# Attention and a Mish FFN in one kernel: two units' probabilities computed with keys on partitions, and a new order of the work

## The chip, the cores and the metric

The kernel runs on one core of one Trainium2 chip. The metric is the device time of one execution in microseconds. In the profile PE is TensorE (PEld its weight loads), DVE VectorE, ACT ScalarE, POOL GpSimd, and SP SyncE, which issues most DMAs.

## What is computed

Attention over 8 batches, 8 heads, 576 tokens and 64 dimensions, four heads with a plain window of 32 tokens, four with every fourth token of a window of 128; then a feed-forward layer on all 4608 tokens, 512 to 2048 to 512, whose weights come as 64-bit floats:

```python
def _attn_ref(q, k, v):
    scores = scale * np.matmul(q, k.transpose(0, 1, 3, 2))
    mask_plain = (rel >= 0) & (rel < window)
    mask_dil = (rel >= 0) & (rel < window * dilation) & (rel % dilation == 0)
    scores = np.where(masks[None, :, :, :], scores, -1000000000.0)
    scores = scores - np.max(scores, axis=-1, keepdims=True)
    attn = np.exp(scores)
    attn = attn / (np.sum(attn, axis=-1, keepdims=True) + 1e-09)
    return np.matmul(attn, v).astype(np.float32)

def _moe_ref(x, w_in, w_out):
    h = x @ w_in
    sp = np.where(h > 20.0, h, np.log1p(np.exp(np.minimum(h, 20.0))))
    g = h * np.tanh(sp)
    return (g @ w_out).astype(np.float32)
```

## The kernel before, in words

The work is cut into 16 **units**, one for each batch and half of the tokens (288 tokens). In a unit the eight heads are four **pairs**: pairs 0 and 1 plain (planar), pairs 2 and 3 dilated. For each pair `scores_of_pair` (step sp) puts a mask product (L650) and q·k (L653) into a double PSUM bank, queries on partitions; `scores` (sc) takes the maximum nm (L683) and, for most pairs, subtracts it (L685); `exps` (ex) does the exponentials; `transpose_p` (tp) brings the probabilities to keys on partitions; `values` (va) multiplies them with v (L801) and divides by the sum (L824, L825); `transpose_x` (tx) brings the result x to the layout of the feed-forward layer, as a half-precision high part (L853) and a low part (L858).

Units 0 to 2 are **direct**: scores in fp32, the probabilities transposed by PE (L778) and copied by ACT into one of two buffers pp (L787). In unit 0 PE itself subtracts the maximum in PSUM (L705) before the exponential (L711); in others a BIASED set does the exponential block by block (L718). From unit 3 on the scores' operands are split into half-precision parts and the probabilities go through a DMA transpose (L771). The feed-forward layer is ff1 (L1054, `ff`), Mish by `gate` (gt, L1069 and L1071), and ff2 (L1081, `fo`), each product as three half-precision ones. From unit 4 on two units share a first layer of seven products for eight, from forms that `w_forms` writes to DRAM (L900 to L918) and `x_forms` makes of x (L939).

The weights pass once through preparation, piece by piece (eight pieces of the first layer, eight of the second): `w_load` (wl), `w_max` (wm, ACT L391, the high words scaled into the place where the weights will stand), `w_scale` (ws, PE L402 and a few small DVE steps), `w_words` (ww, three DVE passes L434, L436, L437 that put a 32-bit float together of the two words; the last sets the sign), `w_split` (wp, ACT L446 and DVE L449). `prep` (pr) finds the scale of v in the direct units by DVE maxima (L334).

The order of everything is one long table, ORDER, of steps by name with a PSUM bank or buffer behind the equals sign, run down once by a loop; a step that is a generator stands in it once for each of its parts. Each engine works through its own instructions in that order, and waits in place. `kw` entries are zero matmuls on PE (`keep_warm`, L1110): there are 328, all ahead of the first ff1. There are four double PSUM banks, four raw weight buffers, two pp and two xs. SP issues the DMAs in the table's order.

Of the kernel before, what the change touches and what calls it, by code (L numbers as in the profile page):

```python
# [35 lines left out]
HI = 2.0 ** -112  # L36
MASKED = -2.0 ** 30
# [17 lines left out]
tp1.3=2 ff0.1=0 va1.2=1 ld2 tp1.3=1 wl1.2.1=0 ww0.1.0 wp0.2.1 wp0.1.0 ff0.1 ff0.1 va1.0=0 wm1.2.1 gt0.3 ww0.1.1
va1.3=2 tp1.1=3 tp1.1=0 ww1.2.1 ff0.5=0 ff0.4=3 ff0.4 va1.2 va1.2=1 wl1.2.0=1 wp0.1.1 tx1.0=1 wm1.2.0 wp0.1.0 ff0.5
ff0.4=2 va1.3 tx1.0 ww1.2.0 ff0.5 ws1.2=3 wp0.1.1 fs1 wl1.3.1=3 va1.3=0 tx1.0 tx1.3=0 tx1.3 tx1.0 ff0.2=2 va1.1=1 pr2
tx1.3 ws1.2 gt0.0=1 va1.1 gt0.0 tx1.3 tx1.2=3 tx1.2 va1.1=0 wl1.3.0=2 ww1.2.1 ff0.2 ff0.2=0 sp2.3=0 sc2.3=1 wm1.3.0
ww1.3.0 wm1.3.1 tx1.2 tx1.1=1 tx1.2 tx1.1 tx1.1 wp1.2.1 wp1.2.1 ff0.3=2 ff0.3 ff1.7=3 ff1.7 sp2.1=1 ff0.3 ex2.3 pr2=2
ww1.2.0 pr2 tp2.3=2 ff1.6=0 gt0.2=5 tp2.3=1 sc2.1=3 ww1.3.1 ex2.1 ws1.3=2 ww1.3.0 wp1.2.0 ff1.6 ws1.3 ff1.6=1 ff1.2=1  # L60
wp1.2.0 ff1.2 gt0.1=0 ff1.7 ff1.3=2 wl1.0.0=0 wl1.0.1=1 wm1.0.0 tp2.1=0 ff1.3 gt0.2 tp2.1=0 va2.1=3 ww1.3.1 sp2.2=0
gt0.1 ff1.2=2 ff1.3 sp2.0=1 fo0.2.0=2 ww1.0.0 fo0.2.1 fo0.2.2 gt1.1=2 va2.1 wp1.3.0 sc2.2=0 va2.1=1 wp1.3.1 va2.3=3
fo0.2.3 ex2.2 wp1.3.0 sc2.0=2 wf1.1=0 wl1.1.1=2 gt1.1 va2.3 wm1.0.1 wm1.1.1 wp1.3.1 ff1.1=0 fo0.2.3=0 wl1.1.0=3
va2.3=0 ww1.0.1 xa2.0=4 ws1.0=3 wf1.1 ex2.0 ff1.1 ws1.0 wf1.1=2 wf1.1 tx2.1=1 wf1.1 ff1.0=3 ww1.1.1 tx2.1 wm1.1.0
ww1.1.0 tx2.1 tx2.1 ww1.0.1 ff1.0 ff1.0=0 ff1.5=1 ff1.1 tp2.2=3 ws1.1=0 tp2.2=0 ff1.4=3 wp1.0.1 ww1.0.0 ff1.5 ff1.4
gt1.0=3 ws1.1 lv3 wp1.0.0 fs2 ff1.4=2 fo0.3.0 ff1.5 gt1.2=6 tx2.3=3 tp2.0=0 ww1.1.0 tp2.0=1 va2.2=1 ww1.1.1 xa2.1=0
# [143 lines left out]
def attn_mish_ffn_kernel(  # L210
# [960 lines left out]
```

## Time and profile before

| what | before |
|---|---|
| median of 3 runs (lowest to highest) | 878.14 us (876.85 to 878.18) |
| the profiled execution, its own time | 878.1 us |
| its span in the profile | 876.3 us |
| busy: PE, DVE, ACT | 864.0 (99%), 684.4 (78%), 674.0 (77%) us |

The span is the stretch that the profile covers; the execution's own time has 1.8 us more around it. A busy time of PE counts matmuls that overlap each other, so the length of a group of matmuls is read best from the start of one group to the start of the next. Many fp32 matmuls stand in the profile as two records each.

### The profile page before, as it was taken

What the parts mean: (1) busy time and instruction counts of PE and PEld (TensorE: products, weight loads), DVE (VectorE), ACT (ScalarE), POOL (GpSimd) and SP (SyncE); (2) the same over time, 40 slices, a digit from 0 to 9 for tenths busy, and PEclk for the clock granted to TensorE, in tenths of its full rate; (3) what the DMA queues carried; (4) which work ended last, traced back from release to release, by engine and by line L of the source; (5) the groups of instructions that cost most, each with busy time, mean ns of one, the idle gap of its engine ahead of it and who ended that gap; (6) DMA issues with size and microseconds to landing.
All of it is one profiled execution on the core that took longest, in us unless ns stands there. A gap on an engine that the chain in (4) does not pass through costs nothing.

```text
span 876.3 us, 21569 instructions
## 1 busy us (share of the span) xinstructions
PE 864.0 (99%) x8992; PEld 696.0 (79%) x8996; DVE 684.4 (78%) x1048; ACT 674.0 (77%) x994; POOL 20.7 (2%) x91
## 2 busy tenths in 40 slices
PE   9999999989999999999999999999999999999998
PEld 8878887777888778877888788777887788877776
DVE  5999999999999898988888598977887587743210
ACT  3688997789888999879996989778887759636412
POOL 1000005000000000000000000000000000000000
PEclk9999999999999999999999999999999999999999
DMA  8674362575578876766987767866685654645201
GB/s 278 215 214 158 130 197 59 156 178 151 129 182 205 208 185 179 177 142 186 208 163 158 205 183 169 196 126 166 182 197 153 174 167 113 133 105 181 82 1 55
DMA packets 210865, 141.20 MB, mean 161 GB/s; under 512 B 151376, under 2 KB 195920, under 8 KB 210768
## 3 DMA queue, kind: packets, MB, share of 16 engines
q1 hardware_dynamic: 210768, 139.83, 61.5%
q8 instruction: 70, 1.15, 0.5%
q14 instruction: 27, 0.22, 0.1%
HBM read 93.06 MB, written 16.78 MB: 125 GB/s over the span
## 4 chain that ended last, share of the span: by engine, by line
PE 67%; ACT 5%; DVE 2%; DMA 2%; issue 1%; SPq 1%; DVEq 0%; ACTq 0%
PE b L1081 35%; PE b L966 23%; PE b L807 3%; PE b L1054 3%; PE b L653 2%; DMA w<-wd 1%; DMA pT<-p 1%; ACT hm L976 1%; ACT sb L724 0%; DVE p L768 0%; ACT k L576 0%; ACT p L766 0%; DVE sb L677 0%; ACT hm L1057 0%; DMA vdn<-in_vd 0%
## 5 line engine op out<-in xcount | busy, mean ns | idle before, releaser
L1081 PE MATMUL b<-g,w 128*128 128x288 f16 x3072 | 391.1, 286 | 0.0
L1081 PEld LDWEIGHTS <-w 128*128 128x128 f16 x3072 | 296.7, 98 | 74.5
L966 PEld LDWEIGHTS <-w 128*128 128x128 f16 x2016 | 195.0, 98 | 52.4 <-issue 1.6
L966 PE MATMUL b<-xf,w 128*128 128x288 f16 x1440 | 210.7, 286 | 1.8 <-DMA w<-wd 0.8
L1054 PE MATMUL b<-xf,w 128*128 128x288 f16 x768 | 101.6, 289 | 2.9 <-DVE g L825 2.2
L1071 DVE SCALAR_TENSOR_TENSOR g<-hm,sg,g 128x1152 f16<-128x1152 f32 x64 | 90.0, 1411 | 17.3 <-ACT g L1069 17.3
L1054 PEld LDWEIGHTS <-w 128*128 128x128 f16 x768 | 74.8, 99 | 22.9 <-DVE g L825 2.5
L1095 ACT ACTIVATE y<-b,fo 128x288 f32<-128x288 f32 x60 | 43.9, 739 | 54.2 <-PE b L1081 44.7
L1069 ACT ACTIVATE g<-hm,sg 128x1152 f16<-128x1152 f32 x64 | 79.9, 1253 | 0.9
L976 ACT ACTIVATE hm<-hm,fs 128x576 f32<-128x576 f32 x72 | 53.9, 770 | 18.8 <-DVE hm L1012 13.4
L966 PE MATMUL b<-w,w 128*128 128x288 f16 x288 | 64.4, 286 | 0.0
L768 DVE TENSOR_TENSOR p<-sb,p 96x768 f16<-96x768 f32 (+3 forms) x52 | 46.7, 904 | 14.0 <-ACT p L766 13.9
L685 DVE TENSOR_TENSOR sb<-sb,nm 96x768 f32<-96x768 f32 (+4 forms) x64 | 49.2, 769 | 2.2
L683 DVE TENSOR_REDUCE nm<-sb 96x6 f32<-96x768 f32 (+4 forms) x64 | 48.8, 763 | 1.8
L724 ACT ACTIVATE sb<-sb,ln_p 96x768 f32<-96x768 f32 (+3 forms) x52 | 46.1, 896 | 5.2 <-DVE sb L685 5.0
L766 ACT CAST p<-sb 96x768 f16<-96x768 f32 (+3 forms) x52 | 41.3, 794 | 3.2 <-DMA pT<-p 2.5
L807 PEld LDWEIGHTS <-pT 128*128 128x128 f16 (+3 forms) x1092 | 39.4, 98 | 2.7 <-DMA out_T<-y 0.3
L1027 DVE TENSOR_TENSOR hm<-b,hm 128x576 f32<-128x576 f32 x24 | 18.1, 752 | 27.5 <-PE b L966 26.8
L966 PE MATMUL b<-xg,w 128*128 128x288 f16 x288 | 39.4, 286 | 0.0
L653 PEld LDWEIGHTS <-q 64*72 64x72 f16 (+1 forms) x1092 | 28.1, 116 | 8.1 <-issue 6.7
L949 ACT CAST w<-w 72x1024 f16<-72x1024 f32 (+3 forms) x27 | 23.3, 867 | 14.4 <-DVE w L940 4.1
L951 DVE TENSOR_TENSOR w<-w,w 72x1024 f16<-72x1024 f32 (+3 forms) x27 | 27.0, 999 | 9.2 <-ACT w L949 9.0
(192 smaller groups left out, 1147.3 us busy)
## 6 DMA issues: line engine op xcount, KB each, us to landing
w<-wd SPq DMA_DIRECT2D x84, 512.0 KB
qn<-in_qT SPq DMA_DIRECT2D x16, 576.0 KB
out_T<-y SPq DMA_DIRECT2D x64, 144.0 KB
raw<-in_w_in SPq DMA_DIRECT2D x16, 512.0 KB
raw<-in_w_out SPq DMA_DIRECT2D x16, 512.0 KB
vn<-in_v SPq DMA_DIRECT2D x48, 128.0 KB
wd<-hm SPq DMA_DIRECT2D x32, 128.0 KB
knd<-in_kdT SPq DMA_DIRECT2D x16, 208.0 KB
```

The costliest lines, as they stand in the source:

```text
L653: nc.tensor.matmul(o, q, k, start=start, stop=stop, skip_group_check=True)
L683: nc.vector.tensor_reduce(nm[:nq, :, j:j + n], x, axis=AX.X, op=ALU.max, negate=True)
L685: nc.vector.tensor_tensor(blocked(sb, c0, n, w), x, nm[:nq, :, j:j + n].unsqueeze(3).broadcast_to([nq, 2, n, w]), op=ALU.add)
L724: nc.scalar.activation(x, x, AF.Exp, bias=ln_p[:nq])
L768: nc.vector.tensor_tensor(lo, src, hi, op=ALU.subtract)
L807: nc.tensor.matmul(avv[:, h, j], pp[:nk, c:c + P], vv[vi][:nk, j, hh, :], start=(i == 0), stop=(i == 2))
L966: nc.tensor.matmul(o[:, h, :HT], t[:, c, wi, h * P:(h + 1) * P], form_of(p, x, c, xi), skip_group_check=True, start=start and n == 0, stop ...
L976: nc.scalar.activation(o, src, AF.Mish, scale=U[2 * p]["fs"][:, j:j + 1])
L1054: nc.tensor.matmul(ph[:, h, :HT], w1[j][c // WIDE][:, c % WIDE, wi, k * P:(k + 1) * P], x_of(d, xi, c), start=(n == 0), stop=(n == len(seq ...
L1069: nc.scalar.activation(g[:, 0], m, AF.Identity, scale=sg)
L1071: nc.vector.scalar_tensor_tensor(g[:, 1], m, sg, g[:, 0], ALU.mult, ALU.subtract)
L1081: nc.tensor.matmul(po[:, :HT], w2[:, e, j, wi, k * P:(k + 1) * P], d["g"][j][:, gi, k, :], start=(j == 0 and n == 0), stop=(j == NCH - 1 a ...
```

## The change

- **Units 0 and 1 (ACROSS).** The maximum nm is still found from scores with queries on partitions. Then `across`, called in place of the transposes, computes the scores once more with keys on partitions: for each block and head a mask product with the mask as weights, a k·q product, and a product whose weights are nm spread over the columns and whose other operand is the unit matrix. The exponential goes from PSUM straight into pp. L705, L778 and L787 of these units, their `ex` steps, L711 and L718 go.
- **Their prep (SUMMED).** The scale of v comes of sums of magnitudes, one ACT pass each for v and the dilated v, in place of DVE maxima.
- **Six weight pieces (SIGNED).** `w_max` is a parametric ReLU with a negative slope, so that the sign goes with the word; the third pass of `w_words` goes; a new step `wa` takes the magnitude on ACT for `w_scale`.
- **`transpose_x`** takes two pairs at once: one copy for the high, one for the low part. There are two more xs buffers.
- **Unit 0's loads**: q in two halves; the first half and the planar k come first on SP, then the first weights.
- **`x_forms`** subtracts half as much in one step.
- **ORDER** is another table: 208 zero matmuls in place of 328, 196 of them ahead of the first ff1, 60 in a row at the start.

```diff
-kw4=1 kw4=2 wl0.0.1=0 kw4=2 kw4=0 kw4=3 xa0.1=0 kw4=1 kw4=2 wl0.0.0=1 kw4=0 ld0 kw4=1 kw4=0 kw4=2 kw4=3 kw4=1 kw4=3
...
-BIASED = {(0, 0), (0, 1), (0, 2), (0, 3), (1, 0), (1, 3), (2, 0), (2, 1), (2, 2), (2, 3), (3, 2), (3, 3)}
-ON_PE = {(0, 0), (0, 1), (0, 2), (0, 3), (1, 0), (1, 2), (1, 3), (2, 1), (2, 2), (3, 3)}
+BIASED = {(2, 0), (2, 1), (2, 2), (2, 3)}
+ON_PE = {(0, 0), (0, 1), (1, 0), (1, 1), (2, 1)}
+ACROSS = {0, 1}
+SUMMED = {0, 1}
+SIGNED = {(0, 0, 0), (0, 0, 1), (0, 3, 0), (0, 3, 1), (0, 2, 0), (0, 2, 1)}
 ON_DVE = {(0, 1), (1, 0), (1, 1), (1, 2)}
-PE_SUBTRACTS = {0}
...
+    xss += [t.rearrange("p h c -> p (h c)")[:, :4 * P].rearrange("p (j k) -> p j k", k=P) for t in sbs[2:]]
...
-        nc.scalar.activation(a, hi.bitcast(F32), AF.Identity, scale=HI)
+        if (k, g, p) in SIGNED:
+            nc.scalar.activation(a, hi.bitcast(F32), AF.Prelu, scale=HI, alpha=-SIGN)
+        else:
+            nc.scalar.activation(a, hi.bitcast(F32), AF.Identity, scale=HI)
+
+    def w_abs(k, g, p):
+
+        lo, _ = raws[k, g, p]
+        nc.scalar.activation(w_dst(k, g, p)[:, :, 0].bitcast(BF16), lo.bitcast(F32), AF.Abs)
...
         nc.vector.scalar_tensor_tensor(lo, lo, 29, a, ALU.logical_shift_right, ALU.bitwise_or)
-        nc.vector.scalar_tensor_tensor(lo, hi, -0x80000000, lo, ALU.bitwise_and, ALU.bitwise_or)
+        if (k, g, p) not in SIGNED:
+            nc.vector.scalar_tensor_tensor(lo, hi, -0x80000000, lo, ALU.bitwise_and, ALU.bitwise_or)
...
+        if u == 0:
+            nc.sync.dma_start(qn[:, :2], qT[b, half, :, :2])
...
+        if d["direct"] and not exact:
+            nc.gpsimd.memset(m, 0.0)
+            unused = take("pp", pps).rearrange("p a t -> p (a t)").bitcast(BF16)
+            for x, o, n in ((d["vn"], m[:, 0:1], P), (d["vdn"][:kd], m[:kd, 1:2], kd)):
+                j, h, e = x.shape[1:]
+                magnitudes(o, x, unused[:n, :j * h * e].rearrange("p (j h e) -> p j h e", j=j, h=h))
+            yield
+            mr = yield from largest(m, 2, u)
...
+        if u in ACROSS:
+            yield from across(u, pair)
+            return
...
+    def across(u, pair):
+
+        d = U[u]
+        bl = blocks(d, 2 * pair)
+        nq = bl[0][0]
+        nm, _ = d.pop(("nm", pair))
+        d.pop(("sb", pair))
+        pt = double(u)
+        mm = lambda *a, **k: nc.tensor.matmul(*a, skip_group_check=True, **k)
+        at = lambda h, x: pt[:x[2], h, x[1]:x[1] + nq]
+        col = 0 if pair < 2 or d["half"] else 2 * P
+        for x in bl:
+            for h in range(2):
+                mm(at(h, x), m_fb[:nq, col:col + x[2]], ident_b[:nq, :nq], start=x is bl[0], stop=False)
+            if pair < 2 and d["half"] == 0:
+                col += x[2]
+        for x in bl:
+            kn, k0 = (d["kn"][0], x[3]) if pair < 2 else (d["kn"][1], x[3] - 2 * d["kw"])
+            for h in range(2):
+                hs = slice(h * D, (h + 1) * D)
+                mm(at(h, x), kn[hs, k0:k0 + x[2]], d["qn"][hs, pair, x[1]:x[1] + nq], start=False, stop=False)
+        for j, x in enumerate(bl):
+            for h in range(2):
+                mm(at(h, x), nm[:nq, h, j:j + 1].broadcast_to([nq, x[2]]), ident[:nq, :nq], start=False, stop=x is bl[-1])
+        yield
+        pp = d["p", pair] = take("pp", pps)
+        w = bl[0][2]
+        for n, a, z in [(QB, 0, QB), (P, QB, HT)] if pair < 2 and d["half"] == 0 else [(w, 0, HT)]:
+            nc.scalar.activation(pp[:n, :, a:z], pt[:n, :, a:z], AF.Exp, scale=1.0 / math.sqrt(D))
...
         if s == 1:
-            tt(a, b, a, op=ALU.subtract)
+            tt(a[:, 0], b[:, 0], a[:, 0], op=ALU.subtract)
```

How the rows stand on three engines. On **PE**, in unit 0: before, behind the scores of a dilated pair (knd, qn), the first planar pair's probabilities (sb) are transposed by the unit matrix.

```order
450 L650 LDWEIGHTS ident_b
451 L650 MATMUL b_74<-m_fb,ident_b 72x288
452 L650 LDWEIGHTS ident_b
453 L650 MATMUL b_74<-m_fb,ident_b 72x288
454 L653 MATMUL b_74<-knd,qn 72x72 x8
455 L778 MATMUL b_73<-ident,sb_84 128x96 x2
456 L778 MATMUL b_73<-ident,sb_84 96x96
```

After, a planar pair of unit 0 (the last of its mask products first):

```order
207 L819 LDWEIGHTS m_fb
208 L819 MATMUL b_72<-ident_b,m_fb 96x96
209 L819 MATMUL b_72<-qn,knp 128x96 x4
210 L819 MATMUL b_72<-qn,knp 96x96 x2
211 L819 MATMUL b_72<-ident,nm 128x96 x4
212 L819 MATMUL b_72<-ident,nm 96x96 x2
213 L1169 LDWEIGHTS zeros
214 L1169 MATMUL b_73<-zeros 128x128
```

In place of six transposes of a pair stand six mask products, six k·q and six products of nm. On **ACT**, from the start of the program, before (raw_76 and raw_77 are the first two weight pieces, m_fb the masks as bf16):

```order
2 L1120 ACTIVATE first<-ln_p 128x1
3 L391 ACTIVATE w_119<-raw_76 128x1024
4 L296 CAST ident_b<-ident 96x96
5 L315 ACTIVATE minus<-ident 128x128
6 L391 ACTIVATE w_118<-raw_77 128x1024
7 L294 ACTIVATE m_fb<-m_f 96x352
8 L446 ACTIVATE w_119<-raw_76,ws_390 128x2x512
```

And after:

```order
3 L392 ACTIVATE w_119<-raw_76 128x1024
4 L296 CAST ident_b<-ident 96x96
5 L315 ACTIVATE minus<-ident 128x128
6 L294 ACTIVATE m_fb<-m_f 96x352
7 L392 ACTIVATE w_118<-raw_77 128x1024
8 L399 ACTIVATE w_119<-raw_76 128x2x512
9 L399 ACTIVATE w_118<-raw_77 128x2x512
```

The masks now stand ahead of the second weight piece, and behind the first as before; the magnitudes of both pieces are new. On **SP**, the loads of unit 4 and its first DMA transpose, before:

```order
55 L1097 DMA out_T<-y_89 128x288
56 L470 DMA qn<-in_qT 128x1152
57 L472 DMA knp<-in_kT 128x2x288
58 L475 DMA knd<-in_kdT 128x4x72 x2
59 L771 DMA_TRANSPOSE pT_2003<-p_2001 128x12x96
60 L496 DMA vn<-in_v 128x256 x3
61 L498 DMA vdn<-in_vd 72x256 x4
```

And after:

```order
55 L485 DMA qn<-in_qT 128x1152
56 L487 DMA knp<-in_kT 128x2x288
57 L494 DMA knd<-in_kdT 128x4x72 x2
58 L1156 DMA out_T<-y_88 128x288
59 L514 DMA vn<-in_v 128x256 x3
60 L516 DMA vdn<-in_vd 72x256 x4
61 L793 DMA_TRANSPOSE pT_2019<-p_2022 128x12x96
```

The loads of v moved ahead of the transpose.

## Rows read from the trace of the kernel before

**Rows 1.** Stretches: busy us of PE, PEld, DVE, ACT, POOL; clock, DMA share, GB/s

```profile
50.00:175.00 125.00, 123.89 (x1198) 100.59 (x1198) 120.84 (x204) 106.78 (x182) 12.59 (x18) 1.00 0.49 148
175.00:205.00 30.00, 27.10 (x300) 21.18 (x299) 28.28 (x58) 25.89 (x41) 0.46 (x5) 0.94 0.67 158
...
235.00:877.00 642.00, 635.68 (x6551) 509.66 (x6548) 468.39 (x684) 488.21 (x698) 4.24 (x49) 1.00 0.63 158
```

**Rows 2.** PE's timeline, 0 to 50: start us, us, operation, records, wait ahead

```profile
1.04 13.01 PE L1110 MATMUL b<-zeros 128*128 128x128 f16 x184 [1.04 <-DVE zeros L1105]
...
14.29 0.85 PE L653 MATMUL b<-knp,qn 64*96 64x128 f32 x12
15.07 1.07 PE L402 MATMUL b<-w,ones 128*128 128x512 bf16 x3
...
17.74 0.74 PE L653 MATMUL b<-knd,qn 64*72 64x72 f32 x16
18.41 0.84 PE L1110 MATMUL b<-zeros 128*128 128x128 f16 x12
19.09 1.40 PE L705 MATMUL b<-nm,ident 96*96 96x256 f32 x8
20.33 0.39 PE L1110 MATMUL b<-zeros 128*128 128x128 f16 x4
...
23.03 0.72 PE L778 MATMUL b<-ident,sb 96*128 96x96 f32 x6
23.58 0.83 PE L1110 MATMUL b<-zeros 128*128 128x128 f16 x12
24.25 1.15 PE L705 MATMUL b<-nm,ident 72*72 72x288 f32 x4
25.24 1.06 PE L1110 MATMUL b<-zeros 128*128 128x128 f16 x16
...
27.62 1.20 PE L801 MATMUL b<-vn,pp 128*96 128x65 f32 x12
28.66 0.17 PE L343 MATMUL b<-m,ones 128*128 128x1 bf16 x1
...
32.97 1.20 PE L801 MATMUL b<-vdn,pp 72*72 72x65 f32 x16
34.00 0.39 PE L1110 MATMUL b<-zeros 128*128 128x128 f16 x4
...
47.64 0.41 PE L856 MATMUL b<-xf,minus 128*128 128x288 f16 x1 [1.06 <-ACT xf L853]
...
48.34 0.94 PE L653 MATMUL b<-knd,qn 64*72 64x104 f32 x16
49.21 0.41 PE L856 MATMUL b<-xf,minus 128*128 128x288 f16 x1
49.45 0.79 PE L1054 MATMUL b<-xf,w 128*128 128x288 f16 x5
```

**Rows 3.** ACT's timeline at the start

```profile
6.01 1.13 ACT L391 ACTIVATE w<-raw 128x1024 f32<-128x1024 f32 x1 [3.78 <-DMA raw<-in_w_in]
...
8.66 1.19 ACT L391 ACTIVATE w<-raw 128x1024 f32<-128x1024 f32 x1 [1.15 <-DMA raw<-in_w_in]
9.72 0.51 ACT L294 ACTIVATE m_fb<-m_f 96x352 bf16<-96x352 f32 x1
```

**Rows 4.** The timeline of all engines around the long wait

```profile
193.11 1.64 PE L1054 MATMUL b<-xf,w 128*128 128x288 f16 x12
...
195.40 1.06 ACT L350 ACTIVATE vdh<-vdn 104x1024 f16<-104x1024 f32 x1 [0.18 <-DMA vdn<-in_vd]
...
196.99 2.50 PE L1054 MATMUL b<-xf,w 128*128 128x288 f16 x12 [2.24 <-DVE g L825]
```

**Rows 5.** Groups of one shape, 0 to 240: the third pass of w_words

```profile
L437 DVE SCALAR_TENSOR_TENSOR raw<-raw 128x1024 int32<-128x1024 int32 x16 | 19.6, 1227 | 0.5
```

**Rows 6.** The page's list of DMA issues: KB of each

```profile
raw<-in_w_in SPq DMA_DIRECT2D x16, 512.0 KB
```

More of the change, by code (lines that the diff above doesn't have):

```diff
@@ L36 @@
 HI = 2.0 ** -112
+SIGN = 2.0 ** 32
 MASKED = -2.0 ** 30
@@ L57 @@
[L57 to L66, printed above, removed]
@@ L469, in loads @@
         qn = d["qn"] = pool.tile([P, 4, HT], F32, tag=tq, name="qn")
-        nc.sync.dma_start(qn, qT[b, half])
+        if u == 0:
+            nc.sync.dma_start(qn[:, :2], qT[b, half, :, :2])
+        else:
+            nc.sync.dma_start(qn, qT[b, half])
         knp = pool.tile([P, 2 * kw], F32, tag="lB", name="knp")
@@ L473, in loads @@
         knd = pool.tile([P, 2 * NR * kd], F32, tag=tk, name="knd")
+        d["kn"] = (knp, knd)
+        if u == 0:
+            yield
+            nc.sync.dma_start(qn[:, 2:], qT[b, half, :, 2:])
         for a in range(2):
@@ L507, in prep @@
         d["f_v"], d["s_v"], d["s"] = f[:, 0:1], s[:, 0:1], s
-        m = pool.tile([P, 6], BF16 if d["direct"] else F32, name="m" if d["direct"] else "mm", bufs=3)
-        if d["direct"]:
+        exact = d["direct"] and u not in SUMMED
+        m = pool.tile([P, 6], BF16 if exact else F32, name="m" if exact else "mm", bufs=3)
+        if d["direct"] and not exact:
[6 more added lines that the diff above has]
+            mr = yield from largest(m, 2, u)
+            m3 = pool.tile([P, 3], F32, name="m3", bufs=3)
+            nc.vector.tensor_reduce(m3[:, :1], mr, axis=AX.X, op=ALU.max)
+            pow2_scales(m3[:, :1], f[:, :1], s[:, :1], TINY / MANY, MANY * 2.0 ** -SPLIT_EXP / 2)
+            eps = d["eps"] = pool.tile([P, 1], F32, name="eps", bufs=4)
+            nc.vector.tensor_scalar(eps, f[:, :1], EPS, None, ALU.mult)
+            return
+        if exact:
             vn, vdn = d["vn"], d["vdn"]
@@ L617, in biased @@
     def biased(u, pair):
-        return u < DIRECT and (u, pair) in BIASED and u not in PE_SUBTRACTS
+        return (u, pair) in BIASED
     def scores_of_pair(u, pair):
@@ L698, in exps @@
         nm, pt = d.pop(("nm", pair))
-        if u in PE_SUBTRACTS:
-            runs = runs_of(d, pair, bl)
-            for h in range(2):
-                j = 0
-                for c0, n, w in runs:
-                    nc.tensor.matmul(pt[:nq, h, c0:c0 + n * w].rearrange("p (j k) -> p j k", k=w), ident[:nq, :nq],
-                                     nm[:nq, h, j:j + n].unsqueeze(2).broadcast_to([nq, n, w]), start=False,
-                                     stop=(c0 == runs[-1][0]), skip_group_check=True)
-                    j += n
-            yield
-            sb = d["sb", pair] = take("sb", sbs)
-            nc.scalar.activation(sb[:nq, :, :width], pt[:nq, :, :width], AF.Exp, scale=1.0 / math.sqrt(D))
-            return
         x = d["sb", pair][:nq, :, :width]
@@ L749, in transpose_p @@
         d = U[u]
-        sb = d.pop(("sb", pair))
         bl = blocks(d, 2 * pair)
         nq, nb, w = bl[0][0], len(bl), bl[0][2]
+        if u in ACROSS:
+            yield from across(u, pair)
+            return
+        sb = d.pop(("sb", pair))
         width = sum(b[2] for b in bl)
@@ L833, in xs_alloc, with transpose_x @@
         U[u]["xs", cp] = t[:QB, :2 * NR * P].rearrange("p (c j k) -> p c j k", c=2, k=P)
-    def transpose_x(u, pair):
+    def transpose_x(u, cp):
         d = U[u]
-        xs = d.pop(("xs", pair))
-        bl = blocks(d, 2 * pair)
-        nq = bl[0][0]
-        px = single(u)
-        for i, (_, q0, _, _, j) in enumerate(bl):
-            if (u, pair) in ON_PE:
-                nc.tensor.matmul(px[:, q0:q0 + nq], xs[:nq, j], ident[:nq, :nq], is_transpose=True, start=(i == 0),
-                                 stop=False, skip_group_check=True)
-            else:
-                nc.tensor.transpose(px[:, q0:q0 + nq], xs[:nq, j], ident[:nq, :nq])
-        yield
-        hi, lo = (x_of(d, i, pair) for i in range(2))
-        src = px[:, :HT]
-        if pair >= 2:
-            hi, lo = (x.rearrange("p (i r) -> p r i", r=NR) for x in (hi, lo))
-            src = src.rearrange("p (r i) -> p r i", r=NR)
+        px = double(u)
+        by_pe = (u, cp) in ON_PE
+        for c in range(2):
+            xs = d.pop(("xs", 2 * cp + c))
+            bl = blocks(d, 4 * cp)
+            nq = bl[0][0]
+            for i, (_, q0, _, _, j) in enumerate(bl):
+                if by_pe:
+                    nc.tensor.matmul(px[:, c, q0:q0 + nq], xs[:nq, j], ident[:nq, :nq], is_transpose=True, start=(i == 0),
+                                     stop=False, skip_group_check=True)
+                else:
+                    nc.tensor.transpose(px[:, c, q0:q0 + nq], xs[:nq, j], ident[:nq, :nq])
+        yield
+        halves = d["x", cp][:, :4 * HT].rearrange("p (c i t) -> p i c t", c=2, i=2)
+        hi, lo = halves[:, 0], halves[:, 1]
+        src = px[:, :, :HT]
+        if cp:
+            hi, lo = (x.rearrange("p c (i r) -> p c r i", r=NR) for x in (hi, lo))
+            src = src.rearrange("p c (r i) -> p c r i", r=NR)
@@ L853, in transpose_x @@
         nc.scalar.copy(hi, src)
         yield
-        if (u, pair) in ON_PE:
-            nc.tensor.matmul(src, minus, hi, start=False, stop=True, skip_group_check=True)
+        if by_pe:
+            for c in range(2):
+                x = halves[:, 0, c]
+                o, x = (px[:, c, :HT], x) if not cp else (px[:, c, :HT].rearrange("p (r i) -> p r i", r=NR),
+                                                         x.rearrange("p (i r) -> p r i", r=NR))
+                nc.tensor.matmul(o, minus, x, start=False, stop=True, skip_group_check=True)
@@ L942, in x_forms @@
             tt(b[:, 1], b[:, 1], a[:, 0], op=ALU.subtract)
-            tt(a[:, 1], a[:, 0], a[:, 1], op=ALU.subtract)
+            tt(a[:, 1], a[:, 1], b[:, 1], op=ALU.subtract)
         yield
```

308 lines of the change are left out of this document (159 added, 149 removed).

## The prediction

> **What bounds the kernel now.** I read the stretches first, then TensorE's timeline up to the first ff1, then the place of the one long wait, and last the forms of the lines that the diff touches. In the stretches [rows 1] PE's column is to be seen against the length: 123.89 of 125 us busy from 50 to 175, 27.10 of 30 from 175 to 205, 635.68 of 642 from 235 on. PE is full, so what PE is given to do shows at the end nearly whole, and what another engine is spared shows only in PE's few gaps. DVE is nearly as full as PE up to 205 us (120.84 of 125, 28.28 of 30), and has room behind (468.39 of 642). Hence a sum of two parts: PE's work, and PE's gaps.
>
> The gaps: 1.1 us in 50 to 175 (125 less 123.89), 2.9 us in 175 to 205, and 6.3 us in the 642 behind 235, spread thin and in the tail. In 175 to 205 the mean clock is also 0.94 [rows 1]: 0.06 of 30 us, 1.8 us more. Its place is one row [rows 4]: PE waits 2.24 us at 196.99 for the DVE's g (L825), and its first twelve ff1 matmuls then take 2.50 us, against 1.64 for twelve at 193.11. So this stall costs 2.9 + 1.8 = 4.7 us. The profiled execution took 878.1 us, equal to the median of 878.14, so the sum is made on 878.1 and stands for the median too; about 0.2% is what a measurement of this kernel can tell from no change.
>
> **PE's work, removed.** Unit 0's subtraction of the maximum (L705): from its start to the next group's start 1.24 us for a planar pair and 0.99 for a dilated one [rows 2], two of each: 4.5 us. The transposes of P (L778) of units 0 and 1: six took 0.55 us [rows 2], and a pair is six or eight smaller ones: eight pairs, 4.4 us. Together 8.9.
>
> **PE's work, added** (across, eight pairs, 56 matmuls of each of three kinds). The k·q products once more, the same count and elements as L653, sides exchanged: 0.78 us for a planar pair, 0.67 for a dilated pair of unit 0, 0.87 for one of unit 1 [rows 2]. Four planar, two and two dilated: 3.1 + 1.3 + 1.7 = 6.2. The mask: 56 bf16 matmuls of 96 or 72 columns. The nearest row is the keep-warm matmul, twelve of 128 columns in 0.68 us, 57 ns each [rows 2]; by columns 43 and 32 ns, 2.1 us in all, without any saving by columns 3.2. I take 2.4.
>
> The broadcast maximum is the disputed price: 56 fp32 matmuls with the maximum as weights, 128, 96, 104 or 72 columns wide, and the unit matrix moving. No row has this form with 128 columns. The nearest are the fp32 products of values (L801): six with mostly 96 weight columns in 1.04 us, 173 ns each, eight with 72 in 1.03, 129 each [rows 2], with fewer moving columns. Their difference grows with the weight columns, 1.8 ns each, so 231 ns for 128 and 187 for 104. Twenty of 128, four of 96, sixteen of 104, sixteen of 72: 4.6 + 0.7 + 3.0 + 2.1 = 10.4. The low end is the transposes' price, 92 ns [rows 2]: 5.2. Between them lies a price by moving columns: L705 moved 704 for a planar pair in 1.24 us, 1.76 ns each, and 24 matmuls of 96 and 32 of 72 would take 8.1. I take the upper one, since the two L801 rows and L705 agree on an fp32 product (173 and 169 ns for 96 columns) and here the weights are the wider side. Prep's maximum by PE: two small matmuls for one, 0.2. Added: 6.2 + 2.4 + 10.4 + 0.2 = 19.2; net of the removed 10.3, low end 5.1.
>
> On this the Trainium skill, page "TensorE: Matmul & The Clock Gate", section "Weight-path perf modes — Fast Weight Load (FWL) and DoubleRow", says that weights come in faster only where 128 are loaded and they are not FP32. By that the change's 128 wide mask weights are the cheap ones and the fp32 maxima get nothing, which speaks for 10.4; no row of before has fp32 weights of 128 columns with a true product.
>
> **Keep-warm and the start.** 328 zero matmuls become 208. At the start 184 stand in a row and take 13.01 us [rows 2], which at 57 ns would be 10.5: the surplus of 2.5 is 44 of them at double time, some 5.0 us at the lower of the clock's two levels (1.2 of 2.4 GHz). After the change 60 stand there: 44 at 114 ns and 16 at 57, 5.9 us, done at 7.0. That saves 7.1; the other 148, against 144, cost 0.2. So PE's work in all: 10.3 − 6.9 = +3.4.
>
> But the first scores then have to be ready at 7.0. Half of q and planar k now stand ahead of the first weights on SP's queue, which is good for them; ACT, however, casts the masks (m_fb) only behind the first weight maximum. That began at 6.01 and the next at 8.66, as the next piece landed [rows 3], which is two DMAs of 512 KB [rows 6]: 1.05 MB in 2.65 us. q's half and k, 0.59 MB, are ahead of it now: later by 1.5 us at that rate, by nothing if they fill time in which nothing came, by 2.65 at worst. ACT: 7.5 + 1.13 for the maximum + about 0.5 for two small casts + 0.51 for m_fb [rows 3] = 9.6. So a **new wait** of 2.6 us (1.1 to 3.8); the mask matmul on PE is in front, and unit 0's k·q, DVE's maxima and the exponentials queue behind it. Against it the old wait of 1.06 us for ACT's copy of x ahead of the first ff1 [rows 2] falls away, since one copy now serves two pairs: −1.1, or nothing.
>
> **Other engines.** DVE loses the third pass over six weight pieces, 1.23 us each [rows 5], 7.4 us; and the maxima of v, the subtractions of unit 1 and the second half of x's subtractions, all less. All lies beside PE; it pays only in gaps. ACT gains an Abs for each of the six pieces, priced as its weight maximum 1.13 [rows 3], 6.8 us, and four sums of v, and loses eight pairs' copies of P and unit 1's exponentials block by block. I take ACT's load as unchanged. The halved subtraction in x_forms lies behind 250 us, where DVE has room [rows 1]: nothing. Paired copies and the Prelu in place of Identity: nothing, the same elements; a switch of activation tables would cost ACT, and the count of them does not change.
>
> **Where the stall goes.** DVE was late with g at 196.99 because it is full and its rec and g wait for the denominators and, on the ACT side, for the magnitudes of unit 5's dilated v, started at 195.40 when their DMA had landed [rows 4]. With at least 7.4 us off DVE ahead of it I expect DVE to be there in time, and in unit 4 the loads of v now stand ahead of the first DMA transpose, which issues them before it waits. So −4.7, and half of the 1.1 us of short waits ahead: −0.5. What is late next is PE itself.
>
> Sum: 878.1 + 3.4 + 2.6 − 1.1 − 4.7 − 0.5 = **877.8**. It is a balance of a larger PE load against a stall, and both ends are wide: own range 875.0 to 880.5.
>
> **Rivals.** *A, the maxima are cheap*: an fp32 matmul with the unit matrix moving costs what a transpose costs, 92 ns. PE's work falls by 5.2: 872.6. For it: the same moving operand. Against it: L801 and L705, whose rows agree on nearly twice that.
>
> *B, the stall stays* (the slower side): one mechanism, ACT. PE's wait at 196.99 goes back over DVE to work that ACT does in order, and ACT, 6.8 us more by Abs, is relieved of copies only in units 0 and 1. If ACT's chain to the magnitudes and denominators of units 4 and 5 is not earlier against PE's ff1 by the 2.24 us of that wait [rows 4], PE stops there, the clock falls again, and the 4.7 are not regained: 882.5. It decides as soon as ACT's net load ahead of 195 grows by over about 2 us. For it: ACT started the magnitudes only 0.18 us after being free [rows 4]. Against it: DVE, not ACT, ended the wait.
>
> *C, DVE sets the pace*: every microsecond off DVE's queue shows. Then −7.4: 870.7. Against it PE's 99% in 50 to 175 [rows 1].
>
> *D, the clock falls at the start*: the 2.6 us of waiting at 7.0 come just after the clock rose, and at 196.99 a wait of 2.24 us was followed by a stretch that cost 1.8 us [rows 1, 4]. That alone is 879.6. The Trainium skill, page "TensorE: Matmul & The Clock Gate", section "What's actually happening", says that the throttled clock is the default and activity releases it: by that the shorter keep-warm run, followed by a wait, would lead here; the same 1.8 us is what it would cost.
>
> **How the numbers follow.** Forecast 0.42 (faster 0.12, same 0.22, slower 0.08 of it, by its range); A 0.18, C 0.08, both faster; B 0.24, nearly all slower; D 0.08, half same and half slower. Faster by over 0.2% means under 876.4, slower over 879.9. Faster 0.38, same 0.28, slower 0.34 (B 0.22, the forecast 0.08, D 0.04). The range holds the forecast, D, B and A: 871.5 to 883.0. Left out are C and the far ends where B and the cheap or dear ends add up.
>
> **What would show it.** In the profile after: the group L819 with the maxima at about 1.3 us for unit 0's planar pair confirms the price, at 0.55 A. The first mask matmul near 9.6 us with PE waiting 2 to 3 us for ACT's m_fb confirms the start; the clock in 5 to 15 us tells D. The first ff1 would stand near 49 us, hardly earlier than 49.45. PE's longest wait between 150 and 230 us gone, with a clock of 1.00, confirms the stall's end; one of over 2 us ended by DVE or ACT there is B. The forecast is wrong if PE's busy time rises by less than 1 or more than 6 us, or if gaps of over 2 us stand elsewhere.

## The result, and the profile after

The changed kernel takes 883.43 us (median of 4 runs, 882.29 to 883.73) against 878.16: the ratio is 1.0059, with a 95% interval of 1.0041 to 1.0076. It is slower by 5.3 us, where 877.8 was forecast with a range up to 883.0. The profiled execution took 883.64 us, its span is 881.9.

The stretches of the kernel after, with the columns of [rows 1]:

```profile
0.00:50.00 50.00, 43.58 (x563) 38.39 (x566) 26.98 (x52) 26.05 (x37) 3.70 (x21) 0.93 0.81 238
50.00:175.00 125.00, 121.77 (x1217) 99.50 (x1218) 112.37 (x192) 102.95 (x160) 10.52 (x18) 1.00 0.46 140
175.00:205.00 30.00, 29.77 (x329) 24.27 (x324) 29.04 (x51) 28.71 (x49) 0.55 (x5) 1.00 0.75 180
...
235.00:882.00 647.00, 643.01 (x6664) 515.52 (x6661) 470.81 (x696) 492.72 (x704) 4.26 (x49) 1.00 0.64 158
```

Three things are to be seen. In 175 to 205 PE is busy 29.77 of 30 us at a clock of 1.00: the stall of [rows 1, 4] is gone. In 50 to 175 its gaps are 3.2 us, not 1.1. And the first 50 us have a clock of 0.93 and 6.4 us without work on PE. The timeline of PE there, to be held against [rows 2]:

```profile
1.05 5.01 PE L1169 MATMUL b<-zeros 128*128 128x128 f16 x60 [1.05 <-DVE zeros L1164]
11.33 0.75 PE L683 MATMUL b<-m_fb,ident_b 96*96 96x352 bf16 x2 [5.27 <-ACT m_fb L294]
12.01 1.49 PE L686 MATMUL b<-knp,qn 64*96 64x128 f32 x12
...
25.00 0.43 PE L819 MATMUL b<-ident_b,m_fb 96*128 96x96 bf16 x6
25.36 0.86 PE L819 MATMUL b<-qn,knp 64*128 64x96 f32 x12
26.15 1.47 PE L819 MATMUL b<-ident,nm 96*128 96x96 f32 x12
27.46 0.44 PE L819 MATMUL b<-ident_b,m_fb 72*72 72x72 bf16 x8
27.83 0.74 PE L819 MATMUL b<-qn,knd 64*72 64x72 f32 x16
28.50 1.26 PE L819 MATMUL b<-ident,nm 72*72 72x72 f32 x16
29.59 0.39 PE L1169 MATMUL b<-zeros 128*128 128x128 f16 x4
...
47.86 1.58 PE L819 MATMUL b<-ident,nm 96*128 96x96 f32 x12
49.27 0.68 PE L915 MATMUL b<-xf,minus 128*128 128x288 f16 x2
...
53.97 3.11 PE L1113 MATMUL b<-xf,w 128*128 128x288 f16 x24
```

The zero matmuls end at 6.06, the first scores start at 11.33, and the first ff1 at 53.97, which stood at 49.45 [rows 2]. Behind it lie 827.9 us of the span, before 826.9. So 4.5 of the 5.6 us by which the span grew are lost ahead of the first ff1. ACT's timeline says what PE waited for [rows 3]:

```profile
9.40 1.12 ACT L392 ACTIVATE w<-raw 128x1024 f32<-128x1024 f32 x1 [7.18 <-DMA raw<-in_w_in]
10.42 0.26 ACT L296 CAST ident_b<-ident 96x96 bf16<-96x96 f32 x1
10.58 0.31 ACT L315 ACTIVATE minus<-ident 128x128 f16<-128x128 f32 x1
10.79 0.48 ACT L294 ACTIVATE m_fb<-m_f 96x352 bf16<-96x352 f32 x1
```

The first weights land 3.4 us later than before, and the masks stand behind them. What the wait does to the clock is in narrower stretches of the kernel after (columns of [rows 1]):

```profile
6.00:11.00 5.00, 0.06 (x2) 0.12 (x1) 0.44 (x1) 1.59 (x4) 0.00 (x0) 1.00 0.99 365
11.00:18.00 7.00, 6.67 (x53) 5.29 (x53) 4.37 (x7) 3.02 (x4) 0.00 (x0) 0.51 1.01 290
18.00:25.00 7.00, 6.95 (x103) 6.08 (x101) 1.73 (x5) 4.36 (x8) 0.00 (x0) 1.00 0.86 235
```

From 6 to 11 us PE does next to nothing; from 11 to 18 it works at 0.51 of the clock, the lower of its two levels, and loses some 3.4 us (an estimate: half of 7 us). The six k·q products at 12.01 take 1.42 us to the next group, where [rows 2] have 0.78.

### The profile page after: what moved, and what is told of

Read it like the earlier page. It is cut to its first block, busy times and chain, and to the rows that moved or that the text cites. A ratio compares the mean times of both kernels' runs of the same rounds, so it can differ in the third digit from the quotient of the medians.

```text
span 881.9 us, 21715 instructions
## 1 busy us (share of the span) xinstructions
PE 867.8 (98%) x9076; PEld 700.9 (79%) x9079; DVE 668.4 (76%) x1034; ACT 676.0 (77%) x978; POOL 19.0 (2%) x93
## 4 chain that ended last, share of the span: by engine, by line
PE 65%; DVE 6%; ACT 4%; issue 1%; DMA 1%; DVEq 0%; ACTq 0%
PE b L1140 33%; PE b L1025 26%; PE b L859 3%; PE b L686 2%; DVE nm L716 1%; DVE sb L710 1%; DVE g L1130 1%; DMA w<-wd 1%; PE b L1113 1%; DVE p L790 1%; ACT sb L743 0%; ACT L743 0%; DVE hm L971 0%; DVE w L1010 0%; DVE g L1010 0%
## 5 line engine op out<-in xcount | busy, mean ns | idle before, releaser
L718 DVE TENSOR_TENSOR sb<-sb,nm 96x768 f32<-96x768 f32 (+4 forms) x64 | 49.2, 769 | 2.2
L1010 DVE TENSOR_TENSOR w<-w,w 72x1024 f16<-72x1024 f32 (+3 forms) x31 | 29.6, 957 | 6.6 <-ACT w L1008 6.6
L1008 ACT CAST w<-w 72x1024 f16<-72x1024 f32 (+3 forms) x31 | 25.8, 836 | 10.5 <-DVE w L999 2.7
```

The lines of the kernel that those rows point to most:

```text
L718: nc.vector.tensor_tensor(blocked(sb, c0, n, w), x, nm[:nq, :, j:j + n].unsqueeze(3).broadcast_to([nq, 2, n, w]), op=ALU.add)
```

## The experiments

The theory after this profile, "start": the change as such comes out near the forecast; what is lost is lost in the first 25 us, by a wait for masks that stand behind late weights, and by the clock. The first rival, "work": PE's added products, or DVE and ACT behind, set the end, and an earlier start is given back.

The kernel before was timed again beside the runs: 878.23 us beside e1 to e4, 877.27 beside e5 to e8, 877.35 beside e9 and e10. Where a run is compared with one of another group, the ratio to the kernel before is the better measure, and is given; the changed kernel's is 1.0059. Lines of ORDER in the diffs are cut out of longer ones.

**e1, masks first.** The casts are issued inside the hand-set order, ahead of the first weight maximum.

```diff
-    nc.scalar.mul(m_fb, m_f, math.sqrt(D))
...
-    nc.scalar.copy(ident_b, ident[:QB, :QB])
...
         nc.scalar.activation(first, ln_p, AF.Exp)
+        nc.scalar.copy(ident_b, ident[:QB, :QB])
+        nc.scalar.mul(m_fb, m_f, math.sqrt(D))
```

> The changed kernel with one edit: ACT casts the unit matrix and the masks (ident_b, m_fb) ahead of the first weight maximum instead of behind it. Theory 'start': the changed kernel loses its time at the start, where PE waits 5.3 us for m_fb and then works 6.8 us at half clock. The first scores then start as soon as planar k has landed. If k landed near 9.4 us (the next DMA on its lane was issued at 9.57), the start moves from 11.3 to 9.5: about 881.6. If k landed by 6.1, where the keep-warm run ends, the whole wait and the clock loss go: about 874.7. Rival 'work': PE's added work and the other engines behind set the end, and an earlier start is given back: 883.4 as it is.

Measured: 879.47 us, 4.0 less than the changed kernel and 1.0012 (0.9999 to 1.0026) of the kernel before. PE's timeline:

```profile
6.01 0.46 PE L681 MATMUL b<-m_fb,ident_b 96*96 96x352 bf16 x2
6.40 0.85 PE L684 MATMUL b<-knp,qn 64*96 64x128 f32 x12
...
12.59 0.42 PE L817 MATMUL b<-ident_b,m_fb 96*128 96x96 bf16 x6 [2.26 <-DVE nm L714]
...
49.74 3.11 PE L1111 MATMUL b<-xf,w 128*128 128x288 f16 x24
```

Planar k was there at 6.4, so the 5.27 us hung on the masks alone. The time lies between the two that were named, since a new wait of 2.26 us came for nm, which stood on DVE behind the first pass over the late weights, and with it some 3.4 us at half clock from 14.7 on. This profiled execution took 880.63 us: its first ff1 is 4.2 us earlier than in the changed kernel, and 3.1 of it arrive at the end of its span (878.8 for 881.9). So most of an earlier start is kept. The executions differ by the clock: five of the twelve were granted 1.000 over the whole program and took 876.7 to 878.6 us, seven were granted 0.996 or 0.998 and took 879.3 to 883.1.

**e2, the wait filled.** Two steps of 47 zero matmuls ahead of the first scores, nothing else.

```diff
-kw4=3 ld0 sp0.1=0
+kw4=3 ld0 kw47=1 kw47=2 sp0.1=0
```

> The changed kernel with 94 more zero matmuls ahead of the first scores, which fill the 5.3 us of PE's wait and move nothing else. Theory 'start': the clock stays at its upper level through the wait, the 6.8 us at half clock are gone, half of them are regained: 880.0. Rival 'work': the same 883.4. If the clock falls although PE is filled, or the matmuls delay the scores, 883 to 884.

Measured: 882.08 us, 1.4 less. Its PE:

```profile
1.05 11.47 PE L1169 MATMUL b<-zeros 128*128 128x128 f16 x154 [1.05 <-DVE zeros L1164]
12.35 0.46 PE L683 MATMUL b<-m_fb,ident_b 96*96 96x352 bf16 x2
...
52.05 3.11 PE L1113 MATMUL b<-xf,w 128*128 128x288 f16 x24
```

The clock stays at 1.00 over the first 50 us. The scores start 1.0 us later than in the changed kernel, and the first ff1 is still 1.9 us earlier: from first scores to first ff1 39.7 us instead of 42.6. So the clock's share is 2.9 us, near the 3.4 expected, in part used up by the later start: the fill ran until the masks had been ready for some 0.7 us (cast on ACT from 11.19 to 11.69). That is why the time lies between the 880.0 of the theory and the 883.4 of the rival.

**e3, maxima in bf16.** A softmax does not depend on the constant taken off, so the rounded maximum serves as well.

```diff
-        nm = pool.tile([QB, 2, 4], F32, name="nm", bufs=4)
+        nm = pool.tile([QB, 2, 4], BF16 if by_pe else F32, name="nb" if by_pe else "nm", bufs=4)
...
-                mm(at(h, x), nm[:nq, h, j:j + 1].broadcast_to([nq, x[2]]), ident[:nq, :nq], start=False, stop=x is bl[-1])
+                mm(at(h, x), nm[:nq, h, j:j + 1].broadcast_to([nq, x[2]]), ident_b[:nq, :nq], start=False, stop=x is bl[-1])
```

> The changed kernel with the row maximum of units 0 and 1 rounded to bf16 and its 56 broadcast products in bf16 (the result of a softmax does not depend on the constant that is taken off, so nothing is left out). The fp32 products take 10.5 us in the changed kernel by start to start; in bf16 they should cost as the mask products do, 0.36 us for six and 0.37 for eight: 2.9 us. Theory that PE's work shows in full at the end: minus 7.6, 875.8. Rival, DVE and ACT pace the first 235 us: minus 0 to 2, 881.5 to 883.4.

Measured: 875.41 us, 8.0 less, although in its profiled execution the masks came 1.4 us later still:

```profile
12.75 0.75 PE L683 MATMUL b<-m_fb,ident_b 96*96 96x352 bf16 x2 [6.44 <-ACT m_fb L294]
...
49.19 3.11 PE L1113 MATMUL b<-xf,w 128*128 128x288 f16 x24
```

PE's work shows in full at the end. DVE and ACT do not pace the stretch to 235 us.

**e4, the third pass back.** No piece is SIGNED, and its step for the magnitude does nothing.

```diff
-SIGNED = {(0, 0, 0), (0, 0, 1), (0, 3, 0), (0, 3, 1), (0, 2, 0), (0, 2, 1)}
+SIGNED = set()
...
     def w_abs(k, g, p):

+        if (k, g, p) not in SIGNED:
+            return
```

> The changed kernel with the weight pieces' signs as before: the third DVE pass back for six pieces (plus 7.4 us on DVE), the plain scaling on ACT, and no Abs steps (minus 6.8 us on ACT); the order of all else stays. The prediction's step: DVE's relief took the stall of 175 to 205 us away; then a wait of over 2 us returns between 100 and 230 us, and the first ff1 comes later where DVE is in front: 886 to 890. Rival: DVE's relief had no part in it, or ACT's load was as much in the way: 882 to 884.

Measured: 884.52 us, 1.1 more. PE's longest waits:

```profile
PE b L685 <- ACT m_fb L294: 4.5, 1, 4.5
PE b L355 <- ACT vdh L350: 1.7, 1, 1.7
PE b L1142 <- DVE w L463: 1.2, 1, 1.2
```

They are those of the changed kernel (5.3, 1.7, 1.2), and in 175 to 205 PE is busy 29.77 us again, at a clock of 1.00. The stall does not come back, so the third pass alone did not make it. The pass is not all of DVE's relief: up to 205 us DVE is busy 187.5 us before, 168.4 in the changed kernel and 174.7 here, so 6.3 of 19.1 us are given back. The exchange of these DVE passes for ACT passes is worth about 1 us, hardly more than the executions of one kernel differ.

**e5, weights first on SP.**

```diff
-kw4=3 ld0 sp0.1=0 wl0.0.1=0 wm0.0.1=0 kw4=1
-wl0.0.0=1 wm0.0.0=0
+kw4=3 wl0.0.1=0 wl0.0.0=1 ld0 sp0.1=0 wm0.0.1=0 kw4=1
+wm0.0.0=0
```

> The changed kernel with one edit in the order of SP's loads: the first two weight pieces ahead of the halved q and planar k, as in the kernel before; the casts of the masks stay behind the first weight maximum. Theory 'start, weights late': what moved ahead of the weights made them land at 9.4 to 10.8 instead of 6.0 and with them the masks. Then the first weight maximum is again near 6.0, m_fb ready near 8.0, the first scores at 8 to 10 (when k has landed), and the end 2 to 4 us earlier: 879.5 to 881.5. Rival: k then lands later than the weights did, the first scores stand at 11 or later: 883 to 885.

Measured: 882.45 us, and 1.0057 (1.0038 to 1.0075) of the kernel before, as good as the changed kernel's 1.0059. The weights are early, as before; the masks are not:

```profile
6.00 1.12 ACT L392 ACTIVATE w<-raw 128x1024 f32<-128x1024 f32 x1 [3.78 <-DMA raw<-in_w_in]
...
9.05 1.12 ACT L392 ACTIVATE w<-raw 128x1024 f32<-128x1024 f32 x1 [1.55 <-DMA raw<-in_w_in]
10.07 0.48 ACT L294 ACTIVATE m_fb<-m_f 96x352 bf16<-96x352 f32 x1
```

That SP's order made the weights late is settled. The casts, which no table orders, went behind the second weight maximum this time, so PE still waited 4.0 us, to 10.61, and then worked at half clock; the expectation had taken the casts' place for fixed.

**e6, maxima ahead of the weight words on DVE**, on top of e1.

```diff
-wm0.0.0=0 ww0.0.1 kw4=1 kw4=2 kw4=3 kw4=1 sp0.0=2 kw4=3 kw4=1 kw4=3 sc0.1 tp0.1=0
+wm0.0.0=0 kw4=1 kw4=2 kw4=3 kw4=1 sp0.0=2 kw4=3 kw4=1 kw4=3 sc0.1 ww0.0.1 tp0.1=0
```

> The changed kernel with the masks cast first (as in e1) and, on DVE, the first pair's maxima ahead of the first pass over the weight words, in front of which they waited until 11.6 us in e1. PE's wait of 2.3 us for nm at 10.3 should go, and with it the 3.4 us at half clock. If that shows at the end: e1's 879.5 less 2.3 and 1.7, 875.5. Rival: the second weight piece, landed near 14 us and then passed through DVE, ACT and PE, holds the first weight scale and the first ff1 anyway, the wait only changes its place: 879.

Measured: 881.01 us, 1.0045 of the kernel before where e1 has 1.0012, with executions from 877.3 to 888.0. They go by the clock: five were granted 1.000 and took 877.3 to 880.3 us, four were granted 0.990 to 0.992 and took 884.5 to 888.0, one lies between. The profiled execution took 885.4 us, so its trace shows the way of the loss, not its usual size:

```profile
17.24 1.02 PE L411 MATMUL b<-w,ones 128*128 128x512 bf16 x3 [2.39 <-ACT w L397]
...
54.43 3.11 PE L1111 MATMUL b<-xf,w 128*128 128x288 f16 x24
```

The wait for nm is gone and stands as one of 2.39 us for the weights' magnitudes, and a half clock follows it from 18.2 to 31.9 us. The wait changed its place, as the rival said, and in this execution its new place was dearer.

**e7, e1 and e3 together.** Both diffs above, nothing else.

> The changed kernel with both edits, masks cast first (e1, about -4.0) and the broadcast maxima in bf16 (e3, -8.0). If the two add: 883.4 - 4.0 - 8.0 = 871.4, under the kernel before by 0.8%. If the earlier scores only run into the weights, which are not earlier, the gains overlap: 874 to 875.

Measured: 872.46 us, 0.9939 (0.9922 to 0.9955) of the kernel before. In per cent of the kernel before that is 1.20 under the changed kernel, where e1 (0.47) and e3 (0.89) have 1.36 together: two separate causes, which nearly add. The clock is 1.00 in every stretch of its profile, and the first ff1 stands at 44.96:

```profile
44.96 3.10 PE L1111 MATMUL b<-xf,w 128*128 128x288 f16 x24 [0.51 <-ACT xf L915]
```

**e8, the kernel before with unit 5's loads of v ahead of the DMA transpose.** Elsewhere the order is the same.

```diff
-ff2.6=3 ld5 pr5 tp3.2=1 pr5 wf2.1=1 va3.2=1
+ff2.6=3 ld5 lv5 pr5 tp3.2=1 pr5 wf2.1=1 va3.2=1
...
-va3.2 va3.3 lv5 pr5
+va3.2 va3.3 pr5
```

> The kernel before with one edit: unit 5's loads of v issued on SP ahead of the DMA transpose that they stood behind (issued at 189.0 and 190.5, behind a transpose of 3.8 us). Theory 'late v': the stall of 2.24 us at 196.99 hung on the late magnitudes of the dilated v; it goes or shrinks, with it the 3.4 us at half clock: 873.5 to 876. Rival 'order of ff1 against g': PE waits there for the DVE's g because the table puts ff1 too early against it, and loads do not matter: 878.

Measured: 876.29 us, 0.9981 (0.9968 to 0.9994) of the kernel before. Around the place of [rows 4]:

```profile
186.94 1.80 SPq L444 DMA_DIRECT2D vdn<-in_vd  x4
...
189.18 1.35 SPq L717 DMA_TRANSPOSE pT<-p  x1
...
193.92 0.91 PE L753 MATMUL b<-vdh,pT 104*128 104x65 f16 x24 [1.68 <-DMA pT<-p]
...
196.68 1.65 PE L1000 MATMUL b<-xf,w 128*128 128x288 f16 x12 [0.38 <-DVE g L771]
```

The wait for g shrinks from 2.24 to 0.38 us, and a wait of 1.68 us for the transpose, now later, takes its place. PE's gaps in 175 to 205 do not shrink (30 less 26.55, 3.4 us, against 2.9 before). But the clock there is 1.00 for 0.94, and the twelve ff1 matmuls take 1.65 us instead of 2.50: two smaller waits left the clock up, where one longer one took it down. g itself is there only 0.3 us earlier (196.68 for 196.99), so the late v was not what held it. DVE's lines of the kernel before show what was:

```profile
194.81 1.22 DVE L912 TENSOR_TENSOR hm<-hm,hm 128x1024 f16<-128x1024 f32 x1
195.95 0.19 DVE L824 RECIPROCAL rec<-den 72x8 f32<-72x8 f32 x1
196.24 0.69 DVE L825 TENSOR_TENSOR g<-b,rec 72x512 f32<-72x512 f32 x1
```

The denominators had been ready since 194.4 on ACT; a product of `w_forms` (L912) stood on DVE ahead of rec and g. In e8 it stands there too. No run took it from there.

**e9, e7 with the weights first on SP (the edit of e5).**

> The kernel of e7 (masks cast first, maxima in bf16) with the first two weight pieces ahead of q's half and planar k on SP. In e5 that made the weights land at 6.0 and 9.05 instead of 9.4 to 10.3 and about 12; in e7 the weights held PE at 15.8 (1.1 us) and DVE's first pass stood in front of the first maxima. If the weights set the pace of the start: 2 us under e7, 870.5. If k, now behind them, holds the first scores by as much: 872 to 874, with PE waiting for knp between 6 and 10 us.

Measured: 873.87 us, 0.9951 (0.9933 to 0.9969) of the kernel before, some 1 us more than e7 by the ratios, whose intervals overlap.

```profile
10.95 0.85 PE L684 MATMUL b<-knp,qn 64*96 64x128 f32 x12 [4.06 <-DMA knp<-in_kT]
```

Now k holds the scores, for 4.06 us, as the rival said. What comes second on SP lands at 9.4 to 11 us, whichever it is; q and k first, as the change has it, is at least not the worse order once the masks are out of the way.

**e10, e7 without the 148 zero matmuls behind the first 60.** All `kw` entries behind the first scores go, as in this line:

```diff
-kw4=1 kw4=2 kw4=3 kw4=1 sp0.0=2 kw4=3 kw4=1 kw4=3 sc0.1 tp0.1=0 kw4=1 xa1.1=0 kw4=3
+sp0.0=2 sc0.1 tp0.1=0 xa1.1=0
```

> The kernel of e7 without the 148 zero matmuls behind the first 60. The prediction counted each keep-warm matmul left out as 57 ns won, whoever else is late. If that holds, 8.4 us go: 864. If they stand where PE would wait for DVE, ACT or the weights anyway, the time is taken by waits, the clock falls in them, and it is the same or slower: 872 to 876.

Measured: 875.54 us, 0.9969 (0.9954 to 0.9983) of the kernel before, where e7 has 0.9939: some 2.6 us more. Its waits of PE:

```profile
PE b L763 <- DVE nb L660: 5.2, 1, 5.2
PE b L357 <- ACT w L343: 3.1, 3, 1.5
```

8.4 us of work are gone (148 at 57 ns). In the first 50 us PE stands still for 10.1 us, where in e7 it did for 5.1, since e7 has waits of 1.2 and 1.7 us at the same places; and the clock there is 0.90, where e7 has 1.00. The first ff1 is 0.9 us earlier than in e7. So most of what keep-warm takes is time that waits and the lower clock take in its place. The profiled execution took 871.4 us, the fastest of ten; what the others lose goes with the clock granted over the whole program: 871.4 and 871.7 us at 0.994, 873.9 and 874.0 at 0.990, 875.5 to 876.2 at 0.986 and 0.985.

## Why the prediction was wrong, point by point

**What bounds the kernel: right.** PE sets the end, and its work shows in full: e3 took 7.6 us of products away by expectation and 8.0 arrived. Rival C, by which DVE sets the pace, is out: e4 gave DVE six passes back and the time rose by 1.1 us.

**PE's added work: right, a little small.** The planar pair of unit 0 took 0.36 + 0.79 + 1.31 us (from 25.00 to 27.46), the dilated one 0.37 + 0.67 + 1.09. The maxima's six products with 128 columns took 1.41 us at 47.86, 235 ns each, where 231 was worked out of L801; rival A's 92 is refuted. The Trainium skill, page "TensorE: Matmul & The Clock Gate", section "Weight-path perf modes — Fast Weight Load (FWL) and DoubleRow", gives no faster load to FP32 weights and to others only where 128 are loaded; the weight loads of this trace agree, which take 143 ns at 72, 170 at 104 and 190 at 128 columns for the fp32 maxima, and 132 at 104 but 98 at 128 for the bf16 masks. The 8.0 us of e3 are not a matter of that load alone: eight products with 72 columns, too few for the faster load in either type, also fell, from 1.09 to 0.30 us. The mask products, 0.36 us for six and 0.37 for eight, sum near 3 us, at the upper end of 2.1 to 3.2 rather than the 2.4 taken.

**The start: the step that failed.** The prediction saw the place, m_fb behind the first weight maximum, but sized the new wait at 2.6 us with a worst case of 3.8, and it was 5.27. The weights landed 3.4 us later, not 1.5: it had priced the 0.59 MB ahead of them at the rate of 8.66 less 6.01 in [rows 3] (396 GB/s), a rate that the transfers first in the program did not reach on the mean of their first 6 us. The same stretch of both kernels, before and then after (last column GB/s):

```profile
0.00:6.00 6.00, 4.96 (x47) 4.96 (x48) 0.19 (x3) 1.49 (x2) 2.84 (x17) 1.00 0.66 221
```

```profile
0.00:6.00 6.00, 4.95 (x60) 4.84 (x60) 0.19 (x3) 1.49 (x2) 2.92 (x19) 1.00 0.64 169
```

With q's half and k in front, 169 GB/s moved instead of 221. And by 9.40 us 2.2 MB had moved in the kernel after, where q's half, k and the first weights are 1.64: loads issued behind the weights, from 3.96 us on, moved beside them (before, 1.3 MB by 6 us, 1.05 of it the weights). How much each of the two made is not measured apart; that the order of SP's loads made the weights late is (e5). The scores started at 11.33, 1.7 us after the 9.6 of the prediction. The other 0.9 us of the wait come of the zero matmuls, done at 6.06 and not at 7.0: the 60 took 5.01 us, where 5.9 was worked out.

**The clock: put in the wrong place.** Rival D had the lower clock after this wait, but as a case apart with 0.08, priced at 1.8 us. It belonged into the forecast: the row that it rested on, 2.24 us of waiting followed by a loss of 1.8 [rows 1, 4], was a warning that a wait of the length forecast can bring it. It was 7 us at half clock, some 3.4 us lost; e2 measured 2.9 back. 1.7 with 2.9 to 3.4 is 4.6 to 5.1, against the 5.0 us by which the first ff1, at 53.97, came later than the prediction's 49. This, and not the work, is the gap of 5.6 us between 877.8 and 883.4, but for about 1 us.

**Rival B's time came by another way.** It said 882.5 by a stall that stays. The time is near it; the mechanism is not, since the stall went.

**The stall's end: right in size, its reason not shown.** 175 to 205 lost its gap and its low clock, as the −4.7 said. Two reasons were given. DVE was in the way, as the lines beside e8 show; but the third pass was not what put it there, since e4 gives it back and the stall stays away. The loads of v moved g by 0.3 us only (e8). What is left is the rest of DVE's relief and the new table, which has the steps of `w_forms` at other places; no run parts the two.

**Short waits: wrong sign.** −0.5 was counted in 50 to 175; PE's gaps grew there from 1.1 to 3.2 us. The wait of 1.06 us for ACT's copy of x did go, as the −1.1 said. The two that came, in the kernel after:

```profile
143.22 10.46 PE L1140 MATMUL b<-g,w 128*128 128x288 f16 x84 [1.24 <-DVE w L461]
155.91 0.27 PE L355 MATMUL b<-ident,mm 128*6 128x128 f32 x1 [1.74 <-ACT vdh L350]
```

The second is ACT's magnitudes of unit 3's dilated v, the kind of work that the prediction had put behind the old stall; here it does hold PE. In 235 to the end the gaps fell from 5.6 to 3.9 us and paid for most of it, which no term had foreseen: luck. (The 6.3 of the prediction counts 0.7 us past the end of the span; no sum used it.)

**Keep-warm: a term that is not free.** −6.9 us was booked for 120 matmuls less, each as 57 ns won. Where they stood ahead of late data the time became a wait. At the start 8.0 us of them went (13.01 less 5.01), and the first scores came only 2.6 us earlier (13.89 before, 11.33 after): 5.27 us became a wait, and the half clock behind it took some 3 us more. In e10 8.4 us more of them went, for 5.0 us more of standing still, a clock of 0.90 and some 2.6 us more at the end.

## What to carry to other kernels

A filler on a busy engine is not work that can be booked as saved: ask what the engine would wait for in its place, and price that wait with the clock behind it. When loads change places at a program's start, price them by what moved in the first microseconds, and look for what else stands behind the load that now comes second, a cast that no table orders included. And where a constant need not be exact, as the maximum under a softmax, a narrower type can be worth more than moving the work: here 8.0 us.

## What the runs showed of the hardware that was not expected

A single wait of 5.27 us by PE was followed by 7 us at half clock, in which PE was busy 6.67 of 7.00 us with small products; in e6 a wait of 2.39 us was followed by 13.7 us, in which PE was never idle. After two waits of 1.68 and 0.38 us in e8 the clock stayed up. The clock is not the same in every execution of one kernel: of e1's twelve, with a wait of 2.26 us in the one that was traced, five kept 1.000. In the first six microseconds the same 16 DMA engines moved 221, 216 and 208 GB/s with the weights first (the kernel before, e5, e9), and 160 to 175 with q's half and k first (the kernel after, e1, e2, e3, e7).
